# Attention and a two-layer MLP on one core: sums of x one by one, buffers of their own for the first product's sums, a stricter count of slots, twelve score groups in range two

## The chip, the cores and the metric

The kernel runs on one core of a Trainium2 chip. The metric is device time in microseconds, of the whole launch. Matmuls run on PE (TensorE), elementwise work on DVE (VectorE) and ACT (ScalarE, which also takes the exponentials and the activation), copies that change type and the loads from memory on POOL (GpSimd), stores and transposing DMAs on SP (SyncE). Each engine works through its own instructions in the order in which the program gives them; between engines semaphores hold an instruction back until what it reads is written and what it overwrites is read.

## The reference

Eight batches of attention with 12 heads, 448 positions and a head width of 64, then an MLP over the 3584 tokens, 768 wide, 2048 inside, with a leaky ReLU:

```python
scores = scale * np.matmul(q, k.transpose(0, 1, 3, 2))
attn = np.exp(scores) / (np.sum(np.exp(scores), axis=-1, keepdims=True) + 1e-09)
x = np.matmul(attn, v).transpose(0, 2, 1, 3).reshape(3584, 768)
h = x @ w_in
out = np.maximum(0.01 * h, h) @ w_out
```

(The maximum that the reference takes off the scores first is left out here.)

## The kernel before

**Attention.** Two heads make a unit; there are 48 units, six to a batch. A unit is loaded by POOL (`load_soft`, L131), cast by POOL (`cast`, L160 for q and k, L162 for v), turned on SP by a transposing DMA (`turn`, L227), and its scores come in four chunks of 112 keys. Three chunks, whatever their units, are a group: six matmuls on PE (`scores`, L261) into three score slots `sc` of PSUM, and three exponentials on ACT (`expo`, L270) into `e`. The value products of a unit are 32 matmuls (`rows`, L798, into a score slot; in the early ranges `pv`, L280, into the banks `g`). DVE divides them by the sum of the exponentials (L804 and L805, or L287 and L288) and so reads the slot out, and SP turns the result into `xT`, whose columns are tokens.

**The MLP.** The tokens are cut into eight ranges of 384 and 512 in turn. From the third on, `hidden` makes the first product and `block_pair` the second. Both replace a product of two by two blocks by seven products of blocks instead of eight, in a scheme of sums: sums of blocks of x (`mix_x`, L381 to L384, on DVE, into `x_mix` and in place into `xT`), of h (`mix_h`, L408 and L409, and L520 and L524), and of the weights, made once. In `hidden` the seven products (L436, six matmuls for each of two columns' halves) run in two chains, one in the banks `g` and one in the score slots; ACT copies a partial sum out of PSUM into a tile (L448, L456, L460), DVE adds to it (L451, L463, L466), and ACT applies the ReLU (L425, the call in `act`). In `block_pair` each of the seven products has eight matmuls of 384 columns (L508), with a place to break off after four; a step is four matmuls. DVE copies or adds the bank into an output tile (`keep` L513, `join` L516, L547), and `store` (L314) sends it out by SP, at the very end by ACT's queue too. The partial sums and the output tiles come from one pool of five buffers, `o_pool`.

**What sets the order.** The first two ranges are `mlp(0)` and `mlp(1)`, and between their steps `cluster` puts one score group each, with the value products, casts, loads and turns that go with it; `begin` says how many: clusters 9 to 18 in range one, 19 to 27 in range two. `due` holds value products that are put off. From the third range on a small planner, `events(i)`, is asked at every step of `block_pair`. It keeps a clock (`now`, 0.65 a step), a time from which each slot is free and a time from which each unit is ready, and then puts a score group (`burst`) or a unit's value products (`rows`) or nothing; `plan` says how many groups each range gets. Between the steps of `hidden` only rows are put. `advance` hands SP and POOL one turn, cast or load at a time, with its counts in `to`. The sums of x for the next range are put as one block of eight on DVE, six steps after the last rows that they need; for the third range they stand ahead of `hidden(2)`. The program's order is kept on each engine.

## Time and profile before

| | us |
|---|---|
| median of 3 runs | 403.18 (402.88 to 403.83) |
| the profiled execution, its own time | 402.84 |
| span of that execution in the trace | 400.9 |
| DVE: sums of x, normalising, copies and adds: busy | 228.9 |
| ACT busy | 261.2 |

A row of a timeline gives the start in microseconds, the duration of a run of like instructions, the engine, the line of the program, the operation, the tile written and the tiles read, the shape and the count; behind it in brackets stands how long the engine was idle before, and the instruction that released it. Names are those of the program: `g` a bank, `sc` a score slot, `h` the hidden layer, `o` an output tile. The costliest groups of the page, as busy time, mean ns of one, and idle time before it with its releaser:

```profile
L270 ACT ACTIVATE e<-sc 112x896 bf16<-112x896 f32 x192 | 163.0, 918 | 51.4 <-PE sc L261 51.0
L508 PE MATMUL g<-w_out_sb,h 128*128 128x384 bf16 x416 | 77.6, 326 | 2.4 <-DVE o L513 2.4
L261 PE MATMUL sc<-qkT 64*128 64x448 bf16 x384 | 52.3, 353 | 3.4 <-DVE x L805 2.8
```

### The profile page before, as it was taken

What the parts mean: (1) busy time and instruction counts of PE and PEld (TensorE: products, weight loads), DVE (VectorE), ACT (ScalarE), POOL (GpSimd) and SP (SyncE); (2) the same over time, 40 slices, a digit from 0 to 9 for tenths busy, and PEclk for the clock granted to TensorE, in tenths of its full rate; (3) what the DMA queues carried; (4) which work ended last, traced back from release to release, by engine and by line L of the source; (5) the groups of instructions that cost most, each with busy time, mean ns of one, the idle gap of its engine ahead of it and who ended that gap; (6) DMA issues with size and microseconds to landing.
All of it is one profiled execution on the core that took longest, in us unless ns stands there. A gap on an engine that the chain in (4) does not pass through costs nothing.

```text
span 400.9 us, 10048 instructions
## 1 busy us (share of the span) xinstructions
PE 383.9 (96%) x4088; PEld 259.0 (65%) x4088; DVE 228.9 (57%) x513; ACT 261.2 (65%) x396; POOL 142.3 (36%) x222
## 2 busy tenths in 40 slices
PE   7999999999999999988999899999999899989995
PEld 3666665545556875567855598578655795658753
DVE  3662663566666683644754646475735665473853
ACT  5998885577445678755878658758787287608600
POOL 8786763657632462543025325352022000000000
PEclk9999999999999999999999999999999999999999
DMA  9999999999994986989058897769128400411022
GB/s 132 195 201 204 203 201 127 144 171 116 130 181 113 123 107 121 150 133 198 2 76 130 159 177 94 102 154 101 25 58 161 116 11 4 113 37 55 2 78 82
DMA packets 96031, 46.98 MB, mean 117 GB/s; under 512 B 52592, under 2 KB 92656, under 8 KB 95984
## 3 DMA queue, kind: packets, MB, share of 16 engines
q0 software_dynamic: 40272, 22.58, 44.2%
q1 hardware_dynamic: 55408, 23.50, 30.4%
q8 instruction: 32, 0.52, 0.6%
q10 hardware_dynamic: 304, 0.25, 0.2%
q14 instruction: 15, 0.12, 0.1%
HBM read 45.61 MB, written 11.01 MB: 141 GB/s over the span
## 4 chain that ended last, share of the span: by engine, by line
PE 53%; DVE 6%; DMA 4%; issue 1%; ACT 1%; SPq 0%; DVEq 0%; ACTq 0%
PE g L508 22%; PE sc L436 10%; PE g L436 10%; PE sc L261 6%; PE sc L798 6%; DMA xT<-x 2%; DMA out_dram<-o 2%; DVE o L513 1%; DVE xT L382 1%; DVE x_mix L383 1%; ACT h L425 1%; DVE x_mix L381 1%; DVE x_mix L384 1%; DVE x L805 1%; DVE h L520 0%
## 5 line engine op out<-in xcount | busy, mean ns | idle before, releaser
L270 ACT ACTIVATE e<-sc 112x896 bf16<-112x896 f32 x192 | 163.0, 918 | 51.4 <-PE sc L261 51.0
L508 PEld LDWEIGHTS <-h 128*128 128x128 bf16 x632 | 57.6, 98 | 45.8 <-issue 13.1
L508 PE MATMUL g<-w_out_sb,h 128*128 128x384 bf16 x416 | 77.6, 326 | 2.4 <-DVE o L513 2.4
L425 ACT ACTIVATE h<-o 128x384 bf16<-128x384 f32 (+1 forms) x72 | 40.6, 576 | 23.5 <-DVE o L451 17.4
L261 PE MATMUL sc<-qkT 64*128 64x448 bf16 x384 | 52.3, 353 | 3.4 <-DVE x L805 2.8
L436 PEld LDWEIGHTS <-w_in_sb 128*128 128x128 bf16 x576 | 52.0, 98 | 5.4 <-issue 1.6
L160 POOL COPY qkb<-fq 112x512 bf16<-112x512 bf16 x38 | 26.3, 692 | 77.8 <-DMA qkT<-qkb 55.6
L162 POOL COPY v<-fv 112x512 bf16<-112x512 bf16 x38 | 24.8, 654 | 64.5 <-PE sc L798 32.3
L436 PEld LDWEIGHTS <-w_in_mix 128*128 128x128 bf16 x432 | 39.1, 98 | 4.6 <-issue 2.2
L508 PE MATMUL g<-w_mix,h 128*128 128x384 bf16 (+1 forms) x216 | 39.8, 320 | 1.0 <-DVE o L513 0.5
L335 PE MATMUL g<-xT,w_in_sb 128*128 128x512 bf16 (+1 forms) x180 | 36.5, 354 | 0.1
L261 PEld LDWEIGHTS <-qkT 64*128 64x128 bf16 x384 | 15.8, 94 | 30.6 <-issue 22.5
L798 PEld LDWEIGHTS <-e 112*128 112x128 bf16 x896 | 31.1, 98 | 5.3 <-ACT e L270 4.2
L798 PE MATMUL sc<-v,e 112*128 112x65 bf16 x896 | 33.4, 194 | 0.1
L516 DVE TENSOR_TENSOR o<-o,g 128x384 f32<-128x384 f32 x39 | 21.5, 551 | 20.4 <-PE g L508 20.2
L160 POOL COPY qkb<-fk 112x512 bf16<-112x512 bf16 x38 | 25.5, 670 | 13.2 <-DMA fk<-in_k_dram 13.0
L280 PEld LDWEIGHTS <-e 112*128 112x128 bf16 x640 | 23.4, 98 | 9.1 <-issue 7.2
L513 DVE COPY o<-g 128x384 f32<-128x384 f32 x39 | 21.6, 553 | 12.2 <-PE g L508 11.8
L335 PEld LDWEIGHTS <-w_in_sb 128*128 128x128 bf16 x192 | 17.9, 97 | 15.8 <-issue 0.4
L436 PE MATMUL g<-xT,w_in_sb 128*128 128x192 bf16 (+1 forms) x216 | 26.6, 259 | 1.3 <-DVE o L451 1.3
L280 PE MATMUL g<-v,e 112*128 112x65 bf16 x640 | 26.9, 194 | 0.5 <-ACT e L270 0.2
L436 PE MATMUL sc<-xT,w_in_sb 128*128 128x192 bf16 (+1 forms) x216 | 26.6, 259 | 0.0
(90 smaller groups left out, 489.9 us busy)
## 6 DMA issues: line engine op xcount, KB each, us to landing
fq<-in_q_dram POOLq DMA_DIRECT2D x19, 224.0 KB, 5.1
fk<-in_k_dram POOLq DMA_DIRECT2D x19, 224.0 KB, 6.5
fv<-in_v_dram POOLq DMA_DIRECT2D x19, 224.0 KB, 6.5
w_in_sb<-in_moe_w_in_dram POOLq DMA_DIRECT2D x4, 768.0 KB, 10.9
w_out_sb<-in_moe_w_out_dram POOLq DMA_DIRECT2D x4, 768.0 KB, 13.4
out_dram<-o SPq DMA_DIRECT2D x7, 336.0 KB, 3.6
out_dram<-o SPq DMA_DIRECT2D x8, 288.0 KB, 3.1
out_dram<-o SPq DMA_DIRECT2D x7, 240.0 KB, 3.1
```

What stands on the lines that cost most here:

```text
L160: by(qk_sb[u][:, x].rearrange("p so h d -> p h so d"), f)
L162: by(v_sb[u % NV][:, :, :, :D], f)
L261: nc.tensor.matmul(ps[:, j, :S], t[j * D:(j + 1) * D, S + c * SC:S + c * SC + P], t[j * D:(j + 1) * D, :S], start=True, stop=True,)
L270: nc.scalar.activation(e[:, :, c, :], sc_t.pop((u, c))[:SC, :, :S], AX.Exp, scale=scale)
L280: nc.tensor.matmul(ps[:, qc, :], e[:, at:at + P], vt[:, j, c, :], start=(c == 0), stop=(c == NSC - 1),)
L335: nc.tensor.matmul(open_t[m][:, :n], w_in_sb[:, kk, ts(m, P)], xT[:, kk, at:at + n], start=(fresh and kk == kks[0]), stop=(kk == KD - 1),)
L425: nc.scalar.activation(hs[:, m:m + 2, cols], x.rearrange("p (m t) -> p m t", m=2), AX.Prelu, alpha=0.01)
L436: nc.tensor.matmul(ps[:, j * nh:(j + 1) * nh], w[:, kk, ts(j, P)], x[:, kk], start=(first and j == 0 and kk == 0), stop=(kk == KH - 1), sk ...
L508: nc.tensor.matmul(ps[:, cols], x[:, m], w[:, m], start=(first and m == 0), stop=(m == MH - 1), skip_group_check=True,)
L513: nc.vector.tensor_copy(o[:, at], ps[:, :NW])
L516: nc.vector.tensor_add(o[:, at], o[:, at], ps[:, :NW])
L798: nc.tensor.matmul(ps[:, j, qc, :], e[:, at:at + P], vt[:, j, c, :], start=(c == 0), stop=(c == NSC - 1),)
```

## The change

It has five parts.

1. `mix_x` becomes a generator, `mix_x_part`, that gives one subtraction at a time. From the third range on one of them is put at a step of `block_pair`, beginning five steps after the rows that its part needs; in range two they stand in the second block pair, and the block ahead of `hidden(2)` is gone.
2. The first product's partial sums have a pool of their own, `c_pool`, with five buffers; `o_pool` has three instead of five and holds output tiles only.
3. The planner counts more strictly: a group of scores is put when its slots are free by 0.05 instead of 0.15, rows hold their slot for 1.25 instead of 1.1, and rows are put only when the next group or the next range needs them. `plan` changes to fit.
4. Range two has twelve score groups instead of nine (`begin`), and the counts that the supply begins with change with it; the cast pool has three buffers instead of four and there are five value buffers instead of six, with v casts held back in `due_v` until no value products are due.
5. The tile that warms PE up lies in `x_mix`. The last product's second half goes to a score slot, and what its bank already holds is copied out ahead and added behind.

```diff
-    cast_pool = ctx.enter_context(tc.tile_pool(name="cast", bufs=4))
+    cast_pool = ctx.enter_context(tc.tile_pool(name="cast", bufs=3))
...
-    o_pool = ctx.enter_context(tc.tile_pool(name="o", bufs=5))
+    o_pool = ctx.enter_context(tc.tile_pool(name="o", bufs=3))
+    c_pool = ctx.enter_context(tc.tile_pool(name="c", bufs=5))
...
-    NV = 6
+    NV = 5
...
-    warm = const_pool.tile([P, 512], BF16)
+    warm = x_mix.rearrange("p x k n -> p (x k n)")[:, :512]
...
+    def mix_x_part(i, ks):
...
-        nc.vector.tensor_sub(t3, xT[:, far, two], xT[:, near, two])
-        nc.vector.tensor_sub(xT[:, near, two], xT[:, near, two], xT[:, near, one])
-        nc.vector.tensor_sub(t2, xT[:, far, two], xT[:, near, two])
-        nc.vector.tensor_sub(t4, xT[:, far, one], t2)
+        for o, x, y in (
+            (t3, xT[:, far, two], xT[:, near, two]),
+            (xT[:, near, two], xT[:, near, two], xT[:, near, one]),
+            (t2, xT[:, far, two], xT[:, near, two]),
+            (t4, xT[:, far, one], t2),
+        ):
+            nc.vector.tensor_sub(o, x, y)
+            yield
...
-                return o_pool.tile([P, DM], F32, name="o")[:, :2 * nh]
+                return c_pool.tile([P, 4 * P], F32, name="c")[:, :2 * nh]
...
         if last:
+            nc.vector.tensor_copy(o2[:, NW // 2:NW], b[:, NW // 2:NW])
             store(o1, token(i, x1), left)
             store(o2, t0, right)
...
+            end = slots[0][:, 0]
+            yield from product(end, h[:, hi, two], t4[:, :, w2], first=True, cols=w2)
+            nc.vector.tensor_add(o2[:, w2], o2[:, w2], end[:, w2])
+            store(o2, t0, w2, (nc.scalar, nc.sync))
...
         mix_h(i, ready.pop())
+        x_sums = mix_x(i + 1)
...
+                if c and x > 2:
+                    next(x_sums, None)
...
-            cast(u + 3 + r)
+            cast(u + 3 + r, (0, 1))
+            due_v.append(u + 3 + r)
+        while due_v and not due:
+            cast(due_v.pop(0), (2,))
...
-    begin = [9, 8 * 2 + 3, 8 * 3 + 4]
+    begin = [9, 8 * 2 + 3, 8 * 3 + 7]
...
-    to = {"turn": 24, "cast": 24, "v": 24, "load": [26, 26, 26]}
+    to = {"turn": 26, "cast": 27, "v": 27, "load": [30, 30, 30]}
...
-        if u < min(NU, to["turn"] + 3, to["load"][0], to["load"][1]):
+        if u < min(NU, to["turn"] + 2, to["load"][0], to["load"][1]):
...
-    plan = [0, 0, 9, 9, 5, 8, 5, 0]
+    plan = [0, 0, 8, 8, 4, 8, 5, 0]
...
-                if want and not blocked and all(t <= now + 0.15 + 0.2 * x for x, t in enumerate(at)):
+                if want and not blocked and all(t <= now + 0.05 + 0.2 * x for x, t in enumerate(at)):
...
-                if whole and at[0] <= now + 0.05 and ready.get(u, 0) <= now + 0.05 and (want or u < HP * (i + 2)):
+                if whole and at[0] <= now + 0.05 and ready.get(u, 0) <= now + 0.05 and (
+                    u <= (chunk + 5) // NSC - NE or u < HP * (i + 2)
+                ):
...
-                    free[id(t)] = now + 1.1
+                    free[id(t)] = now + 1.25
...
-                if not mixed:
-                    fresh = fresh + 1 if rows_done >= HP * (i + 2) else 0
-                    if fresh > 5:
-                        mix_x(i + 1, slice(0, 2))
-                        mix_x(i + 1, slice(2, 3))
-                        mixed = True
+                for y in range(2):
+                    fresh[y] += rows_done >= HP * (i + 2) - 1 + y and 14 * c + x > 4
+                for y, sums in enumerate(x_sums):
+                    if fresh[y] > 4 and next(sums, 0) is None:
+                        break
```

On DVE, in the second product of the seventh range, the sums of x for the last range stood as one block between two copies out of the banks (`L513`, `g_99` and `g_100` are the two banks, `L381` to `L384` the sums):

```order
L516 TENSOR_TENSOR o<-o,g_100 128x384
L513 COPY o<-g_99 128x384
L381 TENSOR_TENSOR x_mix<-xT 128x512
L382 TENSOR_TENSOR xT<-xT 128x2x256
L383 TENSOR_TENSOR x_mix<-xT 128x512
L384 TENSOR_TENSOR x_mix<-xT,x_mix 128x512
L381 TENSOR_TENSOR x_mix<-xT 128x256
L382 TENSOR_TENSOR xT<-xT 128x256
L383 TENSOR_TENSOR x_mix<-xT 128x256
L384 TENSOR_TENSOR x_mix<-xT,x_mix 128x256
L513 COPY o<-g_100 128x384
```

After the change the same place reads (the sums are now L393, the copies L523, the adds L526; `g_102` and `g_103` are the banks):

```order
L523 COPY o<-g_102 128x384
L393 TENSOR_TENSOR x_mix<-xT 128x512
L393 TENSOR_TENSOR xT<-xT 128x2x256
L523 COPY o<-g_103 128x384
L393 TENSOR_TENSOR x_mix<-xT 128x512
L393 TENSOR_TENSOR x_mix<-xT,x_mix 128x512
L526 TENSOR_TENSOR o<-o,g_102 128x384
L393 TENSOR_TENSOR x_mix<-xT 128x256
L393 TENSOR_TENSOR xT<-xT 128x256
L526 TENSOR_TENSOR o<-o,g_103 128x384
```

Two sums stand between any two copies or adds where eight stood at one place.

On PE, at one place of a second product, the last value products of a unit (`L798`, or L827 after) were followed by four matmuls of the second product and then by the scores of the next group (`L261`); before:

```order
L798 MATMUL sc_102<-v_108,e_111 128x65
L508 LDWEIGHTS h
L508 MATMUL g_99<-w_mix,h 128x384
L508 LDWEIGHTS h
L508 MATMUL g_99<-w_mix,h 128x384
L508 LDWEIGHTS h
L508 MATMUL g_99<-w_mix,h 128x384
L508 LDWEIGHTS h
L508 MATMUL g_99<-w_mix,h 128x384
L261 LDWEIGHTS qkT_113
L261 MATMUL sc_101<-qkT_113 128x448
```

After, the end of the stretch between rows and scores (the second product is L518, the scores L262):

```order
L518 LDWEIGHTS h
L518 MATMUL g_103<-w_out_sb,h 128x384
L518 LDWEIGHTS hmix
L518 MATMUL g_102<-w_mix,hmix 128x384
L518 LDWEIGHTS hmix
L518 MATMUL g_102<-w_mix,hmix 128x384
L518 LDWEIGHTS hmix
L518 MATMUL g_102<-w_mix,hmix 128x384
L518 LDWEIGHTS hmix
L518 MATMUL g_102<-w_mix,hmix 128x384
L262 LDWEIGHTS qkT_115
L262 MATMUL sc_105<-qkT_115 128x448
```

Between rows and the next scores there are now at least two steps of four matmuls, and what stands there belongs to two products.

On ACT, at the end of range two, where the copies of the third range's first product begin (`L448`), one group's three exponentials (`L270`) stood there last, with value products and MLP work of PE ahead of them:

```order
L270 ACTIVATE e_112<-sc_103 112x2x448
L270 ACTIVATE e_112<-sc_102 112x2x448
L270 ACTIVATE e_112<-sc_101 112x2x448
L270 ACTIVATE e_112<-sc_103 112x2x448
L448 COPY o<-g_99 128x384
L448 COPY o<-sc_102 128x384
```

After (the exponentials are L271, the copy L458, and it writes a tile `c`):

```order
L271 ACTIVATE e_112<-sc_106 112x2x448
L271 ACTIVATE e_112<-sc_105 112x2x448
L271 ACTIVATE e_113<-sc_104 112x2x448
L271 ACTIVATE e_113<-sc_106 112x2x448
L271 ACTIVATE e_113<-sc_105 112x2x448
L271 ACTIVATE e_113<-sc_104 112x2x448
L271 ACTIVATE e_114<-sc_106 112x2x448
L458 COPY c<-g_102 128x384
```

The last two groups of range two are the last six of these exponentials, and the two groups' scores on PE have 32 value products between them.

More of the change, by code (lines that the diff above doesn't have):

```diff
@@ L372, in mix_w_in, with mix_x @@
             yield
-    def mix_x(i, ks):
+    def mix_x(i):
+        yield from mix_x_part(i, slice(0, 2))
+        yield from mix_x_part(i, slice(2, 3))
+    def mix_x_part(i, ks):
         at = cuts[i] % NX
@@ L544, in block_pair @@
         yield
-        for w in (slice(0, NW // 2), slice(NW // 2, NW)) if last else (left,):
-            yield from product(b, h[:, hi, two], t4[:, :, w], cols=w)
-            nc.vector.tensor_copy(o2[:, w], b[:, w])
-            if last:
-                store(o2, t0, w, (nc.scalar, nc.sync))
-        if not last:
-            store(o2, t0)
+        if last:
+            w1, w2 = slice(0, NW // 2), slice(NW // 2, NW)
+            yield from product(b, h[:, hi, two], t4[:, :, w1], cols=w1)
+            nc.vector.tensor_copy(o2[:, w1], b[:, w1])
+            store(o2, t0, w1, (nc.scalar, nc.sync))
+            end = slots[0][:, 0]
+            yield from product(end, h[:, hi, two], t4[:, :, w2], first=True, cols=w2)
+            nc.vector.tensor_add(o2[:, w2], o2[:, w2], end[:, w2])
+            store(o2, t0, w2, (nc.scalar, nc.sync))
+            return
+        yield from product(b, h[:, hi, two], t4)
+        keep(o2, left, b)
+        store(o2, t0)
         banks.reverse()
@@ L616, in mlp @@
                     next(sums, None)
+                if c and x > 2:
+                    next(x_sums, None)
             yield MH * NW, True
+        for _ in x_sums:
+            pass
     def supply(u):
@@ L663 @@
     due = []
+    due_v = []
     def finish(a, j):
@@ L695, in cluster @@
         if r < 3:
-            cast(u + 3 + r)
+            cast(u + 3 + r, (0, 1))
+            due_v.append(u + 3 + r)
+        while due_v and not due:
+            cast(due_v.pop(0), (2,))
+        if r < 3:
             load(u + 5 + r)
@@ L758 @@
         finish(*due.pop(0))
+    while due_v:
+        cast(due_v.pop(0), (2,))
     for _ in sums:
@@ L855, in events @@
                     now += 1.08
-                    free[id(t)] = now + 1.1
-                    if not want:
-                        break
-                    break
+                    free[id(t)] = now + 1.25
                 break
     for i in range(2, B):
-        if i == 2:
-            mix_x(i, slice(0, 2))
-            mix_x(i, slice(2, 3))
         for step, _ in enumerate(hidden(i)):
@@ L869 @@
                 rows()
-        mixed = i + 1 == B
-        fresh = 0
+        x_sums = [mix_x_part(i + 1, slice(0, 2)), mix_x_part(i + 1, slice(2, 3))] if i + 1 < B else []
+        fresh = [0, 0]
         plans = events(i)
@@ L880 @@
                 used = 0.65
-                if not mixed:
-                    fresh = fresh + 1 if rows_done >= HP * (i + 2) else 0
-                    if fresh > 5:
-                        mix_x(i + 1, slice(0, 2))
-                        mix_x(i + 1, slice(2, 3))
-                        mixed = True
+                for y in range(2):
[3 more added lines that the diff above has]
+                        break
         assert chunk >= min(3 * (START + sum(plan[:i + 1])), NU * NSC), (i, chunk)
-        if not mixed:
-            assert rows_done >= HP * (i + 2), (i, rows_done)
-            mix_x(i + 1, slice(0, 2))
-            mix_x(i + 1, slice(2, 3))
+        assert i + 1 == B or rows_done >= HP * (i + 2), (i, rows_done)
+        for sums in x_sums:
+            for _ in sums:
+                pass
 _INS = ['q', 'k', 'v', 'moe_w_in', 'moe_w_out']
```

## The prediction

> **What bounds the kernel now.** I read the shares of the engines on the page first, then PE's own timeline for its holes, and for each hole the row that ends it: the timelines of DVE, ACT and POOL, the waits and the chain that ended last.
>
> ```profile
> PE 383.9 (96%) x4088; PEld 259.0 (65%) x4088; DVE 228.9 (57%) x513; ACT 261.2 (65%) x396; POOL 142.3 (36%) x222
> ```
>
> PE (the matrix engine) is busy for 96% of the span, and no other engine for more than 65%. So only two things can shorten the kernel: less PE work, or fewer holes in PE's row. The change leaves the PE work as it is (the same 64 groups of scores, the same products), so all that it can win are holes. They are counted from the start of one group to the start of the next, less what the group takes undisturbed; the bracket alone is too small, since the pipe's end is modelled.
>
> **What the change removes.** The profiled execution took 402.84 us; the sum is made against that. The median of the runs is 403.18, 0.34 above it.
>
> *First term: the eight sums of x in one block on DVE.* At each of six places PE waits for a copy or a normalisation that stands behind the block.
>
> ```profile
> 126.37 0.74 PE L261 MATMUL sc<-qkT 64*128 64x448 bf16 x6
> 127.04 1.19 PE L280 MATMUL g<-v,e 112*128 112x65 bf16 x32
> 151.34 1.07 PE sc L798 x32
> 152.42 0.65 PE g L508 x4
> 165.51 0.55 PE L261 MATMUL sc<-qkT 64*128 64x448 bf16 x4
> 166.41 0.37 PE L261 MATMUL sc<-qkT 64*128 64x448 bf16 x2 [0.35 <-DVE x L805]
> 166.71 0.82 PE L508 MATMUL g<-w_out_sb,h 128*128 128x384 bf16 x4
> 310.49 0.35 DVE L381 TENSOR_TENSOR x_mix<-xT 128x384 bf16<-128x384 bf16 x1
> ...
> 312.98 0.55 DVE L513 COPY o<-g 128x384 f32<-128x384 f32 x1
> 311.12 1.46 PE L508 MATMUL g<-w_mix,hmix 128*128 128x384 bf16 x8
> 313.58 1.46 PE L508 MATMUL g<-w_out_sb,h 128*128 128x384 bf16 x8 [1.00 <-DVE o L513]
> 354.17 1.46 PE L508 MATMUL g<-w_mix,hmix 128*128 128x384 bf16 x8
> 357.03 1.46 PE L508 MATMUL g<-w_out_sb,h 128*128 128x384 bf16 x8 [1.40 <-DVE o L513]
> 132.68 0.66 PE L436 MATMUL sc<-x_mix,w_in_mix 128*128 128x192 bf16 x6
> 133.95 0.66 PE L436 MATMUL g<-xT,w_in_sb 128*128 128x192 bf16 x6 [0.61 <-DVE o L451]
> 268.51 0.82 PE L436 MATMUL sc<-x_mix,w_in_mix 128*128 128x256 bf16 x6
> 270.03 0.81 PE L436 MATMUL g<-xT,w_in_sb 128*128 128x256 bf16 x6 [0.71 <-DVE o L451]
> 171.98 0.55 PE L261 MATMUL sc<-qkT 64*128 64x448 bf16 x4
> 173.66 0.36 PE L261 MATMUL sc<-qkT 64*128 64x448 bf16 x2 [1.13 <-DVE x L805]
> 222.55 0.55 PE L261 MATMUL sc<-qkT 64*128 64x448 bf16 x4
> 224.40 0.37 PE L261 MATMUL sc<-qkT 64*128 64x448 bf16 x2 [1.30 <-DVE x L805]
> ```
>
> The undisturbed sizes first: a group of scores takes 0.67 (126.37 to 127.04), the two last matmuls of one that waited 0.30 (166.41 to 166.71), a product of eight 1.30 (four take 0.65 in the chain's row at 152.42); by the column that is 0.65 for six matmuls of 256 columns and 0.49 for six of 192. The block at 310.49 reads best: eight subtractions, the next copy out of a bank only at 312.98, and PE's group at 313.58 has waited for it. The holes in time's order: from 132.68, 1.27 - 0.49 = 0.78; from 171.98, 1.68 + 0.30 - 0.67 = 1.31; from 222.55, 1.85 + 0.30 - 0.67 = 1.48; from 268.51, 1.52 - 0.65 = 0.87; from 311.12, 2.46 - 1.30 = 1.16; from 354.17, 2.86 - 1.30 = 1.56. Together **7.2**. After the change one sum (0.35 by the row at 310.49) stands at a step of four matmuls, so two at a product of 1.30, with 0.55 for its copy or join: 1.25 of 1.30, and the bank is due only one product later. So I let these holes go whole; what is late next is DVE itself where a normalisation comes on top, priced below.
>
> *Second term: scores that come too soon behind rows.* "Rows" are the 32 value products, a group of scores has six matmuls and needs three score slots.
>
> ```profile
> 153.00 0.88 PE L261 MATMUL sc<-qkT 64*128 64x448 bf16 x6
> ...
> 342.24 0.88 PE L261 MATMUL sc<-qkT 64*128 64x448 bf16 x6
> ```
>
> Between ranges two and seven 18 of the 36 groups take 0.14 more (0.88 against 0.74 at 126.37; 153.00 is the first, 342.24 the last): their third slot still holds the rows, which DVE reads out. The order before puts one step (0.65, at 152.42) between rows and scores there, the order after always two or more, so the third slot is wanted 0.65 later, against 0.14 missing. That is 18 x 0.14 = 2.5, and the group at 165.51, 1.20 - 0.67 = 0.53: **3.0**. Where DVE has two sums more between, it reads the rows out some 0.7 later, and this gain is half lost; that is in the small waits below.
>
> *Third term: the output's buffers.* Twice the first product's copy on ACT needs a buffer whose store is still out.
>
> ```profile
> 184.14 0.82 PE L436 MATMUL g<-x_mix,w_in_mix 128*128 128x256 bf16 x6
> 185.79 0.82 PE L436 MATMUL sc<-x_mix,w_in_mix 128*128 128x256 bf16 x6 [0.83 <-ACT o L456]
> 187.66 0.81 PE L436 MATMUL sc<-xT,w_in_mix 128*128 128x256 bf16 x6 [0.40 <-ACT o L460]
> ACT o L456 <- DMA out_dram<-o: 1.5, 1, 1.5
> 179.73 7.19 DMA out_dram<-o
> ```
>
> 185.79 - 184.14 - 0.65 = 1.0; the group at 187.66 is the second after 185.79 and would stand at 185.79 + 2 x 0.65 = 187.09: 0.57. Together **1.6**. With buffers of their own the copies wait for DVE and ACT alone. The price would be in the outputs, which keep three buffers of five: the second pair's second tile needs the buffer of the first pair's first tile at its fourth product, so five products after the store's issue at least, 6.5 us, and this store, the one that held the chain, took 7.19. I take nothing, and as an upper bound one store late by 0.7.
>
> *Fourth term: the end.*
>
> ```profile
> 395.28 0.82 PE L508 MATMUL g<-w_mix,h 128*128 128x192 bf16 x8
> 396.55 0.82 PE L508 MATMUL g<-w_mix,h 128*128 128x192 bf16 x8 [0.45 <-DVE o L547]
> 396.53 1.64 ACTq L314 DMA_DIRECT2D out_dram<-o  x2
> ```
>
> 1.27 - 0.65 = 0.6 of hole goes (eight matmuls of 192 columns, half of a product); but the first half's stores issue until 396.53 + 1.64, and the last issue may then wait for its queue. I take **0.45**, between 0.3 and 0.6. The added copy of a partial sum (192 columns, half of the 0.55 at 312.98, some 0.3) lies beside the product before.
>
> The four terms make 7.2 + 3.0 + 1.6 + 0.45 = **12.2**.
>
> **What the change adds.** *Three more score groups in range two*, of which two pairs follow each other with few value products between, at the ends of range two's two block pairs (about 110 to 133 us).
>
> ```profile
> 126.83 2.53 ACT L270 ACTIVATE e<-sc 112x896 bf16<-112x896 f32 x3 [2.66 <-PE sc L261]
> 128.46 0.67 PE L280 MATMUL g<-v,e 112*128 112x65 bf16 x16 [0.23 <-DVE x L288]
> ```
>
> The exponentials of the group at 126.37 end 0.46 + 2.53 = 2.99 after its scores begin, and a following group uses the third slot 0.45 after its own begin (two thirds of 0.67); so two groups must lie 2.54 apart. In the first pair 48 value products lie between (0.67 + 1.5 x 1.19 = 2.45, short by 0.1; a value product also waits for DVE as at 128.46, 0.23): 0.4 with both and some more for the late exponential. In the second pair there are 32: 0.67 + 1.19 = 1.86, short by 0.7, and the 0.23 again: 0.9. Behind it the first product of the next range starts with ACT's copies queued behind the six exponentials: 0.5 to 0.9, I take 0.7. Sum **+2.0**; nothing at all if the exponentials are early, and 3 if each comes whole. The 2.5 us of exponentials themselves are no gain elsewhere, for ACT has room.
>
> *Small waits of the new order.*
>
> ```profile
> L805 DVE TENSOR_TENSOR x<-sc,rec 112x512 bf16<-112x512 f32 x28 | 19.4, 692 | 1.0
> ```
>
> A normalisation (0.69) beside two sums and a copy makes 1.94 of DVE in a product that rows stretch to 1.30 + 1.07 = 2.37; without that stretch it is 0.64 over. I take **+0.8**, one such place, between 0 and 3 (five of them).
>
> Other edits are put at nothing: POOL's and SP's supply (cast buffers three for four, value buffers five for six) has room by its rows below; the warm tile only changes its address.
>
> So 402.84 - 12.2 + 2.0 + 0.8 = 393.4, and with part of the median's 0.34 **393.6**.
>
> One row speaks for a further cost of spreading the sums.
>
> ```profile
> 129.46 1.09 POOL L162 COPY v<-fv 112x512 bf16<-112x512 bf16 x1
> 130.11 0.65 DVE L382 TENSOR_TENSOR xT<-xT 128x384 bf16<-128x384 bf16 x1
> ```
>
> One sum took 0.65 where the row at 310.49, of the same shape, has 0.35, beside a copy on POOL. Forty-eight sums lie in the six ranges; if one in eight is stretched by 0.30, that is 1.8 us of DVE, and a third of it on PE is inside the 0.8. If POOL holds one in two, it is 7.2 us, and half of it on PE would be 3.6 us, so 397. By the Trainium skill ("SBUF — State Buffer", section "SBUF: two separate sides") a DVE operation with two SBUF inputs and a GpSimd operation that reads SBUF exclude each other for the whole instruction. By that rule spread sums, which meet more copies than a block does, would come to the second of the two figures, 397; the trace shows the stretch in these rows, 0.30, and not how often it would come.
>
> **The rivals.** *Costs stay at nothing* (0.08): 402.84 - 12.2 = 390.6.
>
> *Spread sums still hold PE* (0.15). DVE works in order, and a sum that needs a transposed tile holds every copy behind it. For it: a transpose in flight has held the chain for 7.5 us.
>
> ```profile
> 163.51 7.50 DMA xT<-x
> ```
>
> Against it: that row is the longest of the chain, and the first sums begin five steps behind the rows that they need, 3.25 us and whatever rows (1.07) or scores (0.67) lie between, some 5 us, and the copy behind has a product's room, 1.30. So a landing like that one costs 7.5 - 5 - 1.3 = 1.2, a shorter one nothing. If 0.6 to 0.8 reach PE in each of five ranges, the time is about 397; with the stretch by POOL (3.6) it is the same, and both have this chance together.
>
> *Supply in range two comes late* (0.12).
>
> ```profile
> L131 POOL DMA_DIRECT2D fq<-in_q_dram x5: 701/701/703, 68.1 to 108.4; - x5
> 74.96 1.24 PE L335 MATMUL g<-xT,w_in_sb 128*128 128x512 bf16 x5
> ```
>
> Loads of a pair of units went out every (108.4 - 68.1) / 4 = 10.1 us. Range two lasts from 74.96 to its last value products at 128.46, 54 us, for nine groups or 6.75 units (four thirds of a group are a unit). Twelve groups are nine units; three groups and 2.25 units of value products more (3 x 0.67 + 2.25 x 1.19) make it 58.7 us, 6.5 per unit, while the loads come at 5.0 per unit. That is room, but the buffers are fewer and a late unit stops PE outright. Two to five us late: 396 to 398.
>
> *Slower* (0.04): the same supply as the bound. If the three cast buffers and the deferred value casts hold the loads to over 15.2 us a pair (7.6 per unit), range two grows by 9 x (7.6 - 6.5) = 9.9 and eats the gain; at 16 us a pair it is 9 x 1.5 = 13.5, and the time is about 407. From 10.1 that is far. *The order is not what the planner thinks* (0.04): slots come free elsewhere and the second term turns into waits as large, with all else as forecast: 393.6 + 3.0 + 3.0 = 399.6.
>
> **How the numbers follow.** The forecast has 0.57, with a range of its own of 391.5 to 395.5; costs at nothing 0.08, the rivals at 396 to 398 0.27, 399.6 and slower 0.04 each. The range that leaves two in ten out runs from 390.6 to 398.0. A measurement of this kernel tells about 0.2% (0.8 us) from no change: faster by more 0.92, within 0.03, slower by more 0.05.
>
> **What would show it.** Right: no sum of x behind which PE waits at the six places; all 36 score groups behind ranges two to seven at 0.67; ACT's copies without a wait for the output; the two halves of the last product 0.65 from start to start; new holes at the score groups and first products between 110 and 133 us, some 2 us in all. Wrong: holes before score groups of range two that a transpose or a cast ends (supply); sums that wait for the transposes of x, with PE behind them; holes at the stores' buffers in the second products.

## The result and the profile after

The changed kernel takes 393.52 us (median of 4 runs, 392.70 to 394.67) against 403.21 for the kernel before: the ratio is 0.976, with a 95% interval of 0.9733 to 0.9787. Run again beside later experiments it had 0.9773 (0.9743 to 0.9803). The ratios are taken over the runs within 1.5% of a kernel's fastest, which leaves out two of the twelve of one kernel below (ten groups). The profiled execution took 393.48, 9.36 less than the one before; the forecast for it was 393.4.

The page of the changed kernel, shares of the engines first, then, from its waits (us in total, times, longest), PE's for the exponentials ahead of rows:

```profile
PE 381.0 (97%) x4088; PEld 257.4 (66%) x4088; DVE 230.5 (59%) x517; ACT 260.6 (67%) x396; POOL 144.6 (37%) x222
PEld L827 <- ACT e L271: 6.2, 20, 0.7
```

No wait of ACT for a store is left among its waits. The first thing to look for in PE's timeline is the last place of the block of sums, where the kernel before had its hole of 1.56. The start of one product to the start of the next is 1.30 again, and only a small hole stands one product earlier:

```profile
343.85 1.46 PE L518 MATMUL g<-w_mix,h 128*128 128x384 bf16 x8
345.51 1.46 PE L518 MATMUL g<-w_out_sb,h 128*128 128x384 bf16 x8 [0.20 <-DVE o L526]
346.81 1.46 PE L518 MATMUL g<-w_mix,hmix 128*128 128x384 bf16 x8
```

345.51 - 343.85 - 1.30 = 0.36 comes from an add that stands on DVE behind a normalisation and a sum of h. Such a hole is not new: the kernel before had one of 0.37 two products ahead of the 1.56 (the twelve matmuls ahead of it begin at 349.25 and take 1.95, and the next begins at 351.57, released by a copy of DVE).

The end of the kernel, on PE, after the change:

```profile
386.35 0.82 PE L518 MATMUL g<-w_mix,h 128*128 128x192 bf16 x8
387.01 0.82 PE L518 MATMUL sc<-w_mix,h 128*128 128x192 bf16 x8
```

The two halves follow each other in 0.66, not 1.27. But from the last group's start to the end of the span it is 391.7 - 387.01 = 4.69, where it was 400.9 - 396.55 = 4.35 before: 0.34 of the 0.61 is given back behind PE.

The new holes are where the added groups stand, in range two: at the end of its first block pair and at its very end (PE, then ACT):

```profile
116.86 1.20 PE L281 MATMUL g<-v,e 112*128 112x65 bf16 x32
118.28 0.74 PE L281 MATMUL g<-v,e 112*128 112x65 bf16 x16 [0.22 <-DVE x L289]
...
131.05 0.74 PE L262 MATMUL sc<-qkT 64*128 64x448 bf16 x6
131.72 1.35 PE L281 MATMUL g<-v,e 112*128 112x65 bf16 x32
133.00 0.65 PE L262 MATMUL sc<-qkT 64*128 64x448 bf16 x4
134.09 0.36 PE L262 MATMUL sc<-qkT 64*128 64x448 bf16 x2 [0.44 <-ACT e L271]
135.41 0.66 PE L446 MATMUL sc<-xT,w_in_sb 128*128 128x192 bf16 x6
136.52 1.20 PE L827 MATMUL sc<-v,e 112*128 112x65 bf16 x32 [0.45 <-ACT e L271]
...
131.51 4.95 ACT L271 ACTIVATE e<-sc 112x896 bf16<-112x896 f32 x6 [2.96 <-PE sc L262]
```

At the first place the value products wait for DVE, 118.28 - 116.86 - 1.07 = 0.35 (1.07 is what 32 value products took in the chain before). At the second, six exponentials run without a pause from 131.51, and PE waits for them twice: the last two matmuls of the second group begin at 134.09, 1.09 after 133.00, where 0.45 would do; and the rows at 136.52 come 1.11 after 135.41 instead of 0.49.

One hole was in no expectation, at the beginning of the third range's second product:

```profile
152.49 1.47 PE L518 MATMUL g<-w_out_sb,h 128*128 128x384 bf16 x8
154.50 0.81 PE L518 MATMUL g<-w_mix,h 128*128 128x384 bf16 x4 [0.54 <-DVE o L523]
```

154.50 - 152.49 - 1.30 = 0.71. The last experiment is about it.

### The profile page after: what moved, and what is told of

It reads as the page before. It is cut to its first block, busy times and chain, and to the rows that moved or that the text cites. A ratio compares the mean times of both kernels' runs of the same rounds, so it can differ in the third digit from the quotient of the medians.

```text
span 391.7 us, 10029 instructions
## 1 busy us (share of the span) xinstructions
PE 381.0 (97%) x4088; PEld 257.4 (66%) x4088; DVE 230.5 (59%) x517; ACT 260.6 (67%) x396; POOL 144.6 (37%) x222
## 4 chain that ended last, share of the span: by engine, by line
PE 78%; DMA 7%; POOL 5%; issue 4%; DVE 3%; ACT 2%; DVEq 0%; POOLq 0%; ACTq 0%
PE g L518 27%; PE g L446 12%; PE sc L446 11%; PE sc L262 8%; PE sc L827 7%; PE g L336 6%; PE g L281 3%; PE g L581 3%; DMA w_mix<-in_v_dram 3%; DMA fv<-in_v_dram 2%; DMA w_in_mix<-in_k_dram 2%; POOL qkb L161 1%; POOL v L163 1%; ACT h L435 1%; ACT e L271 1%
## 5 line engine op out<-in xcount | busy, mean ns | idle before, releaser
L271 ACT ACTIVATE e<-sc 112x896 bf16<-112x896 f32 x192 | 162.7, 917 | 56.2 <-PE sc L262 56.0
L518 PEld LDWEIGHTS <-h 128*128 128x128 bf16 x632 | 57.8, 98 | 44.6 <-issue 11.5
L518 PE MATMUL g<-w_out_sb,h 128*128 128x384 bf16 x416 | 78.3, 326 | 0.3 <-DVE o L526 0.2
L435 ACT ACTIVATE h<-c 128x384 bf16<-128x384 f32 (+1 forms) x72 | 40.6, 576 | 22.5 <-DVE c L461 14.8
L161 POOL COPY qkb<-fq 112x512 bf16<-112x512 bf16 x38 | 28.2, 743 | 72.2 <-DMA qkT<-qkb 56.5
L262 PE MATMUL sc<-qkT 64*128 64x448 bf16 x384 | 49.5, 353 | 1.1 <-DVE qkT L251 0.6
L518 PE MATMUL g<-w_mix,h 128*128 128x384 bf16 (+1 forms) x208 | 38.5, 323 | 0.7 <-DVE o L523 0.5
L523 DVE COPY o<-g 128x384 f32<-128x384 f32 x51 | 28.2, 553 | 13.0 <-PE g L518 12.6
L827 PEld LDWEIGHTS <-e 112*128 112x128 bf16 x832 | 28.4, 98 | 6.5 <-ACT e L271 6.2
L827 PE MATMUL sc<-v,e 112*128 112x65 bf16 x832 | 31.1, 194 | 0.5 <-ACT e L271 0.5
L526 DVE TENSOR_TENSOR o<-o,g 128x384 f32<-128x384 f32 x39 | 21.5, 551 | 14.6 <-PE g L518 14.5
L262 PEld LDWEIGHTS <-qkT 64*128 64x128 bf16 x384 | 14.7, 94 | 23.3 <-issue 14.8
L281 PE MATMUL g<-v,e 112*128 112x65 bf16 x704 | 29.6, 194 | 0.4 <-DVE x L289 0.2
```

The costliest lines, as they stand in the source:

```text
L161: by(qk_sb[u][:, x].rearrange("p so h d -> p h so d"), f)
L262: nc.tensor.matmul(ps[:, j, :S], t[j * D:(j + 1) * D, S + c * SC:S + c * SC + P], t[j * D:(j + 1) * D, :S], start=True, stop=True,)
L271: nc.scalar.activation(e[:, :, c, :], sc_t.pop((u, c))[:SC, :, :S], AX.Exp, scale=scale)
L281: nc.tensor.matmul(ps[:, qc, :], e[:, at:at + P], vt[:, j, c, :], start=(c == 0), stop=(c == NSC - 1),)
L435: nc.scalar.activation(hs[:, m:m + 2, cols], x.rearrange("p (m t) -> p m t", m=2), AX.Prelu, alpha=0.01)
L518: nc.tensor.matmul(ps[:, cols], x[:, m], w[:, m], start=(first and m == 0), stop=(m == MH - 1), skip_group_check=True,)
```

## The experiments

Each kernel is told by its ratio to the kernel before, since the runs of that one went from 402.45 to 403.83 (medians) between the chips. Spans are those of one profiled execution each; the changed kernel had 391.7 and, when run again, 391.5. The intervals reach 0.7 to 2.1 us to each side, so a difference of under 1 us between two ratios can't be told from none without the traces.

| kernel | ratio (95%) | span, us |
|---|---|---|
| the change | 0.9760 (0.9733 to 0.9787) | 391.7 |
| the change, again | 0.9773 (0.9743 to 0.9803) | 391.5 |
| the change, sums in a block | 0.9810 (0.9787 to 0.9833) | 394.4 |
| the change, one pool of five buffers | 0.9784 (0.9764 to 0.9803) | 392.8 |
| the change, old planner | 0.9777 (0.9757 to 0.9796) | 392.9 |
| the change, old end | 0.9753 (0.9737 to 0.9770) | 392.3 |
| before, sums one at a time | 0.9836 (0.9784 to 0.9888) | 392.1 |
| the change, block and old planner | 0.9959 (0.9931 to 0.9986) | 398.3 |
| the change, nine groups and old planner | 0.9824 (0.9782 to 0.9865) | 395.6 |
| the change, twelve groups placed earlier | 0.9746 (0.9715 to 0.9777) | 389.7 |
| the change, ten groups | 0.9962 (0.9929 to 0.9995) | 405.4 |
| the change, eleven groups | 0.9811 (0.9779 to 0.9844) | 392.0 |
| earlier groups, copies by DMA | 0.9735 (0.9706 to 0.9765) | 390.1 |

### One part put back at a time

The sums in one block:

```diff
-                for y, sums in enumerate(x_sums):
-                    if fresh[y] > 4 and next(sums, 0) is None:
-                        break
+                if fresh[1] > 5:
+                    for sums in x_sums:
+                        for _ in sums:
+                            pass
```

(and in range two the two lines that put single sums are taken out)

> The changed kernel with the eight sums of x of a range in one block again, six steps after the last rows that they need, and for the third range behind range two's second block pair; all else as changed. Theory (the block on DVE holds PE, 7.2 us at six places): 393.5 + 7.2 = 400.7, from 399 to 402, with a hole of 0.8 to 1.6 us at each of the six places, ended by DVE. Rival (the gain is in the other edits, and with them DVE has room enough for a block): under 395.5.

Measured: 396.15 us, 1.5 to 2.0 over the changed kernel by the ratios (0.9810 less 0.9773 and 0.9760) and 2.7 to 2.9 by the spans. Neither end: the block costs something, but not 7.2. The timelines say why. This is the last place (PE), as bad as it was:

```profile
349.25 1.46 PE L518 MATMUL g<-w_out_sb,h 128*128 128x384 bf16 x8
352.12 1.46 PE L518 MATMUL g<-w_mix,h 128*128 128x384 bf16 x8 [1.40 <-DVE o L526]
```

And this is the fourth range, where the kernel before lost 1.48 at 222.55 (DVE, then PE):

```profile
213.07 0.35 DVE L393 TENSOR_TENSOR x_mix<-xT 128x384 bf16<-128x384 bf16 x1
...
215.81 0.69 DVE L832 TENSOR_TENSOR x<-sc,rec 112x512 bf16<-112x512 f32 x1
...
213.87 1.20 PE L825 MATMUL sc<-v,e 112*128 112x65 bf16 x32
214.91 0.81 PE L518 MATMUL g<-w_mix,h 128*128 128x384 bf16 x4
215.56 0.81 PE L518 MATMUL g<-w_out_sb,h 128*128 128x384 bf16 x4
216.30 0.74 PE L262 MATMUL sc<-qkT 64*128 64x448 bf16 x6
```

The eight sums are there from 213.07 on, and the normalisation of the rows stands behind them and ends at 216.50. But with the strict planner two steps lie between the rows and the next scores, and the third slot is wanted only at 216.30 + 0.45 = 216.75. The block is hidden. At one step it would have been wanted 0.65 earlier. The other places lie between: 0.49 and 0.78 are lost at the beginning of the third range's first product (137.84 to 140.09), 0.61 in its second (at 167.42), 0.45 at the beginning of the sixth range's first product (at 262.22), and nothing at the place of the old 313.58. On the other side, the changed kernel's 0.71 at 154.50 isn't there.

The partial sums and the outputs in one pool again:

```diff
-    o_pool = ctx.enter_context(tc.tile_pool(name="o", bufs=3))
-    c_pool = ctx.enter_context(tc.tile_pool(name="c", bufs=5))
+    o_pool = ctx.enter_context(tc.tile_pool(name="o", bufs=5))
...
-                return c_pool.tile([P, 4 * P], F32, name="c")[:, :2 * nh]
+                return o_pool.tile([P, DM], F32, name="o")[:, :2 * nh]
```

> The changed kernel with the first product's partial sums and the outputs in one pool of five buffers again. Theory (two waits of ACT's copies for a store, 1.0 and 0.57): 393.5 + 1.6 = 395.1, from 394.3 to 396, with PE waiting for ACT's copies at the beginning of a first product, and those for a store. Rival (these two waits were accidents of one execution's transfers, or the other edits already moved the stores): within 0.5 of 393.5.

Measured: 394.95 us, 0.4 to 1.0 over the changed kernel by the ratios (0.9784 less 0.9773 and 0.9760), 1.1 to 1.3 by the spans. One wait for a store that holds PE is back, in another range than before (the waits, then PE):

```profile
ACT o L457 <- DMA out_dram<-o: 1.6, 1, 1.6
239.82 0.66 PE L445 MATMUL sc<-xT,w_in_sb 128*128 128x192 bf16 x6
241.60 0.66 PE L445 MATMUL g<-x_mix,w_in_mix 128*128 128x192 bf16 x6 [1.12 <-ACT o L457]
```

241.60 - 239.82 - 0.49 = 1.29. A shared pool makes such a wait possible, not sure: the kernel below with the split alone shares it too, and its waits name no store.

The planner's old numbers:

```diff
-                if want and not blocked and all(t <= now + 0.05 + 0.2 * x for x, t in enumerate(at)):
+                if want and not blocked and all(t <= now + 0.15 + 0.2 * x for x, t in enumerate(at)):
...
-                    u <= (chunk + 5) // NSC - NE or u < HP * (i + 2)
+                    want or u < HP * (i + 2)
...
-                    free[id(t)] = now + 1.25
+                    free[id(t)] = now + 1.1
```

> The changed kernel with the planner's old numbers (0.15, 1.1, rows also when groups are still wanted), but the new numbers of groups for each range. 19 score groups then stand one step behind rows instead of none. Theory (third slot late by 0.14): 19 x 0.14 = 2.7, so 396.2, from 395.5 to 397.5, and the groups take 0.80 to 0.84 again. Rival (it is the smaller number of groups in the later ranges that brought the gain): under 394.5, the groups at 0.67.

Measured: 394.78 us, between the theory and the rival: 0.2 to 0.7 over by the ratios, 1.2 to 1.4 by the spans. The mechanism is as expected: 19 of the groups of scores take 0.87 or 0.88 in PE's timeline from 150 us on and 14 take 0.74, while in the changed kernel all 33 take 0.74. 19 x 0.14 = 2.7 should be lost, and only half of it or less is. Some of it is a trade. With two steps ahead of the scores, the rows stand close behind them, and PE waits for their exponentials (the waits of this kernel, to hold against the 6.2 and 20 above):

```profile
PEld L827 <- ACT e L271: 4.4, 16, 0.7
```

That is four waits and 1.8 of weight loads' idle time, part of it beside matmuls. In PE's own timeline, summed from start to start from the third range's second product on, 2.5 more is lost behind the 33 groups of scores (2.64 for 0.11) and 0.75 less ahead of the 21 rows that stand behind the second product (0.82 for 1.57). So the trade leaves 1.8 by the trace, of which the spans show 1.2 to 1.4; the rest isn't settled.

The old end (the last product's second half in the first's bank):

```diff
-            end = slots[0][:, 0]
-            yield from product(end, h[:, hi, two], t4[:, :, w2], first=True, cols=w2)
-            nc.vector.tensor_add(o2[:, w2], o2[:, w2], end[:, w2])
...
+        for w in (slice(0, NW // 2), slice(NW // 2, NW)) if last else (left,):
+            yield from product(b, h[:, hi, two], t4[:, :, w], cols=w)
+            nc.vector.tensor_copy(o2[:, w], b[:, w])
```

(and the copy ahead is taken out)

> The changed kernel with the last product's second half in the bank of the first again. Theory: the hole of 0.6 on PE is back, and the last store lands 0.3 to 0.6 later: 393.8 to 394.1. Rival (the issue of the first half's stores sets the end in both): no difference, the hole is back but the span from PE's last matmul to the end is shorter by as much.

Measured: 393.86 us, ratio 0.9753 beside 0.9760 and 0.9773: no difference that can be told. The spans differ by 0.6 to 0.8, but the runs don't show it. In its trace the hole is back (386.68 to 387.95, 1.27 for 0.66), and from the last group's start to the end it is 392.3 - 387.95 = 4.35 again. So the trace has the theory's hole and a part of what the rival names, a shorter way to the end: the change of the end is worth 0.61 - 0.34 = 0.27 there; whether it is worth anything in the time stays open.

The four parts put back alone cost 1.5 to 2.0, 0.4 to 1.0, 0.2 to 0.7 and nothing by the ratios: less than half of the 9.7. So the parts don't add up, and the next three kernels ask how.

### How the parts work together

The first part alone, in the kernel before (the changed kernel's generator and its places for the sums; nothing else):

> The kernel before with the first part of the change alone: the sums of x one at a time, as the changed kernel places them. With the block put back, the changed kernel lost 2.0 us, not 7.2. Theory A (two of the six holes are removed by the split and by other parts alike, so that each alone is enough): here all six holes go, ratio to before 0.982 to 0.986 (5.6 to 7.2 us faster), with no hole of over 0.5 behind a sum of x. Theory B (the sums held PE for 2 us only, and the rest came by other parts): ratio 0.994 to 0.996.

Measured: ratio 0.9836 (0.9784 to 0.9888), 6.6 us faster, with runs from 393.86 to 397.86 (the profiled execution was the fastest of the four, by 2.0, so the span in the table flatters this kernel). That is theory A: the split alone removes the six holes. But for the old end's 0.61, the longest that PE has left from the third range on is 0.41, at a group behind rows (171.22).

The block and the planner's old numbers, both put back:

> The changed kernel with the block of sums and the planner's old numbers together. If parts add up: 2.0 + 0.7, ratio 0.983 (from 0.981 to 0.985). If the planner's stricter count is what removed the holes that the block made at 222.55 (1.48) and 313.58 (1.16) and half of the one at 173.66: these are back, ratio 0.988 to 0.993.

Measured: 401.22 us, ratio 0.9959 (0.9931 to 0.9986), 7.5 to 8.0 us over the changed kernel, where the two alone cost 1.5 to 2.0 and 0.2 to 0.7. That is more than either expected range allows. Of the holes that were expected the one at the place of the old 313.58 is back:

```profile
308.82 1.46 PE L518 MATMUL g<-w_mix,hmix 128*128 128x384 bf16 x8
311.30 1.46 PE L518 MATMUL g<-w_out_sb,h 128*128 128x384 bf16 x8 [1.01 <-DVE o L523]
```

311.30 - 308.82 - 1.30 = 1.18. Behind rows PE waits for a copy at 265.30 too (0.49), and the third range has 0.60 and 0.31; but in place of the old 1.48 in the fourth there is only 0.27. So a block on DVE costs PE when something stands close behind it, and the strict planner removes much of what stands close: the spread of the sums removes the holes whole, the strict count more than half of them, and put back one by one the two look small. The spans say the same with less: 394.4 and 392.9 alone, 398.3 together, where the two alone would add up to 395.7. How much of the larger figure of the ratios is more than the spread of the runs (400.09 to 402.56, the fastest of them profiled) isn't settled.

Nine groups in range two with the planner's old numbers:

```diff
-    begin = [9, 8 * 2 + 3, 8 * 3 + 7]
+    begin = [9, 8 * 2 + 3, 8 * 3 + 4]
...
-    plan = [0, 0, 8, 8, 4, 8, 5, 0]
+    plan = [0, 0, 9, 9, 5, 8, 5, 0]
```

(with the counts `to` of the kernel before, and the planner's numbers as two kernels above)

> The changed kernel with nine score groups in range two and the planner's old numbers, nine, nine, five, eight and five groups in the ranges after (the strict count finds no room for so many). Theory (twelve groups cost 1.3 us at range two's end and gain only what the planner's count needs): the two places at range two's end are gone (1.3 to 1.7 faster), the late third slots are back (1.0 slower, as the old numbers alone showed): ratio 0.974 to 0.977. Rival (twelve groups in range two carry most of the gain that the other parts put back one by one don't explain, some 6 us): ratio 0.985 or more.

Measured: 395.67 us, ratio 0.9824 (0.9782 to 0.9865): neither, 2.1 to 2.6 us slower than the changed kernel. (Its profiled execution was the slowest of the four, by 1.5.) The price is in DVE, and then on PE, at the fifth range:

```profile
256.63 0.42 DVE L393 TENSOR_TENSOR x_mix<-xT 128x512 bf16<-128x512 bf16 x1 [2.89 <-DMA xT<-x]
...
256.89 0.55 PE L262 MATMUL sc<-qkT 64*128 64x448 bf16 x4
258.42 0.36 PE L262 MATMUL sc<-qkT 64*128 64x448 bf16 x2 [0.97 <-DVE x L834]
```

A sum of x waits 2.89 for a transpose, the normalisation of the rows stands behind it (at 257.68), and the scores behind that. It is the rival of the spread sums that hold PE, in another kernel than the one it was named for.

### Range two, and a version that is faster than both

The groups of range two put earlier:

```diff
-        total = MD * KD * n + 2 * 7 / 4 * MD * DM
+        total = (MD * KD * n + 2 * 7 / 4 * MD * DM) * (0.92 if i else 1)
```

> The changed kernel with range two's twelve groups put a little earlier (the total of work by which they are placed is taken 8% smaller), so that seven instead of six stand in its first product and one instead of two behind each other at its end. Theory (two groups behind each other at range two's end cost PE 0.14 + 0.18 + 0.70 + 0.61 by the changed kernel's timeline): 1.2 to 1.6 faster than the changed kernel beside it, no hole of over 0.3 between 128 and 138. Rival (the supply bounds range two: units are wanted every 5.0 us there, as fast as the loads come): no gain or a loss, with holes before scores or value products that a cast or a turn ends.

Measured beside the changed kernel on one chip: 391.93 us (391.5 to 393.08, 6 runs) against 393.21 (392.49 to 393.9, 6 runs), 1.28 faster, as the theory has it but for one clause: a hole of a little over 0.3 is left. PE at range two's end now:

```profile
131.97 1.20 PE L281 MATMUL g<-v,e 112*128 112x65 bf16 x32
133.39 0.66 PE L446 MATMUL g<-xT,w_in_sb 128*128 128x192 bf16 x6 [0.22 <-DVE x L289]
```

One group stands there (at 131.30, ahead of these value products), the hole left is 133.39 - 131.97 - 1.07 = 0.35, and the supply follows although the groups come closer. The rival falls.

The changed kernel beside it:

> The changed kernel itself once more, as the measure for the three beside it: ratio to before 0.973 to 0.979.

Measured: 0.9773, within.

Ten groups in range two (`begin` 8 * 3 + 5, `plan` 8, 8, 4, 8, 7 for ranges three to seven) and eleven (8 * 3 + 6; 8, 8, 4, 8, 6), with the counts `to` that belong to them:

> The changed kernel with ten groups in range two and seven in the seventh range instead of five. Theory (a group costs nothing in the seventh range, and the pair of groups at range two's very end is gone, while that at the end of its first pair of blocks has 32 value products between instead of 48): 0.3 to 1.3 faster than the changed kernel beside it. Rival (DVE's sums and rows in the seventh range leave no room for two more groups): slower by 0.3 or more, with holes behind 300.

> The changed kernel with eleven groups in range two and six in the seventh range. Theory: one pair at range two's first end is gone, worth 0 to 0.4, the pair at its very end stays: 0 to 0.4 faster than the changed kernel beside it. Rival as with ten groups: slower.

Measured: ten groups 401.81 us (397.73 to 407.2), ratio 0.9962; eleven 394.46 us, ratio 0.9811, 1.25 over the changed kernel beside them. Both theories fall. The rivals are right that it is slower, but not why: with eleven groups PE has no hole of over 0.2 in the seventh range. The holes are in the fourth and fifth (eleven groups; waits, DVE, then PE; the first DVE row is the changed kernel's, for comparison):

```profile
DVE x_mix L393 <- DMA xT<-x: 13.1, 6, 3.3
232.97 0.69 DVE L834 TENSOR_TENSOR x<-sc,rec 112x512 bf16<-112x512 f32 x1
...
247.89 0.69 DVE L834 TENSOR_TENSOR x<-sc,rec 112x512 bf16<-112x512 f32 x1
...
254.18 0.85 DVE L393 TENSOR_TENSOR x_mix<-xT 128x512 bf16<-128x512 bf16 x1 [3.31 <-DMA xT<-x]
...
253.91 0.81 PE L518 MATMUL g<-w_out_sb,h 128*128 128x384 bf16 x4
255.55 0.81 PE L518 MATMUL g<-w_mix,h 128*128 128x384 bf16 x4 [0.82 <-DVE o L526]
```

Six sums wait for transposes, 13.1 us in all; the changed kernel's waits have no such line. The add that releases PE at 255.55 stands on DVE behind the sum of 254.18. The reason is the lead of the scores. The first sum for the sixth range needs the rows of the 35th unit, which is whole with 140 chunks. By `begin` and `plan`, 47 groups or 141 chunks are done when the fifth range begins with twelve groups, 46 or 138 with eleven, 45 or 135 with ten. So in the changed kernel those rows are put in the fifth range's first product, and their normalisation begins at 232.97, 21 us ahead of the sum (at 254.18 too). With eleven groups they come only in the second product, at 247.89, and the sum five steps behind them waits for a transpose that is still on its way, until 254.18. The kernel with nine groups and the old numbers has 138 chunks there as well: its normalisation begins at 250.63, and the sum waits until 256.63.

The profiled execution with ten groups is the slowest of its twelve (407.2), so its sizes don't hold for the others. It fails in the same way: five of its sums wait for transposes, 11.1 in all, PE itself waits 3.73 for one, at 266.37, and there holes stand behind 300 too.

### Sums beside copies on POOL

The last kernel is the one with earlier groups, and in it the q and k copies of units 28 and 29 are made by DMAs:

```diff
-                by(qk_sb[u][:, x].rearrange("p so h d -> p h so d"), f)
+                o = qk_sb[u][:, x].rearrange("p so h d -> p h so d")
+                if u in (28, 29):
+                    for y in range(2):
+                        nc.gpsimd.dma_start(out=o[:, y], in_=f[:, y])
+                else:
+                    by(o, f)
```

> The kernel with range two's groups put earlier, with the q and k copies of units 28 and 29 made by DMAs that POOL issues instead of by POOL itself. In the kernel without this, four such copies lie between 144.7 and 150.1, beside DVE's sums of h, of which four took 0.64 to 1.24 instead of 0.42, and PE then waits 0.92 at 152.57. Theory (the copies on POOL stretch the sums, and these hold PE): sums of h between 144 and 152 back at 0.42 to 0.45 where only DMA issues lie beside them, the hole at the beginning of the third range's second product under 0.4, and 0.3 to 0.8 faster than the 391.9 of the kernel without it (ratio 0.973). Rival (the sums are slow for another reason, or the late activations on ACT set that hole): sums still over 0.6 and the hole 0.7 or more.

The same stretch without the DMAs (earlier groups; POOL, DVE, PE):

```profile
148.73 0.62 POOL L161 COPY qkb<-fq 112x512 bf16<-112x512 bf16 x1
149.28 0.83 POOL L161 COPY qkb<-fk 112x512 bf16<-112x512 bf16 x1
148.40 1.24 DVE L418 TENSOR_TENSOR hmix<-h 128x512 bf16<-128x512 bf16 x1
149.74 0.64 DVE L419 TENSOR_TENSOR h<-h 128x512 bf16<-128x512 bf16 x1
150.34 1.47 PE L518 MATMUL g<-w_out_sb,h 128*128 128x384 bf16 x8
152.57 1.46 PE L518 MATMUL g<-w_mix,h 128*128 128x384 bf16 x8 [0.76 <-DVE o L523]
```

And with them:

```profile
148.05 1.41 POOL L164 DMA_DIRECT2D qkb<-fk  x2
150.15 0.63 POOL L168 COPY v<-fv 112x512 bf16<-112x512 bf16 x1
149.34 0.43 DVE L423 TENSOR_TENSOR hmix<-h 128x512 bf16<-128x512 bf16 x1
150.21 0.86 DVE L423 TENSOR_TENSOR hmix<-h 128x512 bf16<-128x512 bf16 x1
151.51 1.47 PE L523 MATMUL g<-w_out_sb,h 128*128 128x384 bf16 x8
152.92 1.46 PE L523 MATMUL g<-w_mix,h 128*128 128x384 bf16 x8
```

Seven of the eight sums take 0.42 or 0.43; the one that meets the copy left on POOL, at 150.15, takes 0.86. The hole on PE shrinks from 152.57 - 150.34 - 1.30 = 0.93 to 0.11. The theory holds for the cause. It fails for the time: 392.11 us, ratio 0.9735 beside 0.9746, no difference that can be told. In its profile a hole of 0.67 stands in range two at 109.83 that the kernel without has not, which is about what was won; whether the DMAs cause it was not tried.

## Why the prediction was right, step by step

**The time.** 393.4 was worked out for the profiled execution, and it took 393.48. The sum is that good because it was made for all parts together, from holes that are in fact gone, and both of its halves come out in PE's timelines. Of the 12.2 that were to go, all went: the six holes (7.2), 2.7 behind the groups of scores and the 0.53 at 165.51, the two waits for a store (1.6) and 0.27 at the end make 12.3. Against the 2.8 that were to come stand 2.9: 1.5 in range two, 0.71 at 154.50 and 0.7 ahead of rows. The spans differ by 400.9 - 391.7 = 9.2. But the terms are not what each part is worth by itself.

**The block of sums, 7.2.** Right in the size and the mechanism: the six holes are gone, and the part alone in the kernel before brings 6.6 (4.5 to 8.7). What the prediction didn't see is that the second term's planner would have removed more than half of them by itself: with the strict count the block costs 1.5 to 2.9. One size in the working was small: a sum of 512 columns takes 0.42 where the working took 0.35 from one of 384, so two of them and a copy make 1.39 of a product's 1.30; PE shows no hole for it.

**Scores behind rows, 3.0.** The mechanism is right, all 33 groups are at 0.67 again (three of the 36 are now in range two). Put back alone it is worth less: the old numbers cost 0.2 to 0.7 by the ratios and 1.2 to 1.4 by the spans. The step that failed is the one that let 18 x 0.14 go without a price. What came in exchange, PE's waits for exponentials ahead of rows (0.87 in all before, 1.57 after, from the third range's second product on), was in no term.

**The output's buffers, 1.6.** Right in kind, on the high side: with one pool a wait of 1.29 is back, and the time is 0.4 to 1.0 longer; but the split alone had already moved the two waits of before away. That three output buffers cost nothing was right.

**The end, 0.45.** The hole of 0.61 is gone on PE, 0.34 of it comes back behind PE, so 0.27 by the trace and nothing measurable in the time.

**Range two's groups, +2.0.** 1.8 by the trace: 0.35 at the first pair, and 0.21 at 133.00, 0.64 at 134.09 and 0.62 at 136.52 at the second; 1.5 when the 0.35 that range two's end had before (128.46 - 127.04 - 1.07) is taken off. The kernel that takes the second pair apart is 1.28 faster. For the first pair 0.4 was set, part of it for late exponentials; there the wait for DVE is all, and behind it the exponentials are not late.

**Small waits, +0.8.** Too small, 1.4 by the trace: 0.71 at 154.50, and the 0.7 ahead of rows. The one at 154.50 has a cause that the prediction had only for sums of x: sums of h stretched by POOL's copies. Five of them take 0.64 to 0.83 there; the cause was tried in the kernel with earlier groups, not in the changed kernel itself. For the sums of x the open question is answered: nine of the 48 are stretched in the changed kernel, by 2.65 us in all, nearer to the prediction's one in eight (1.8) than to its one in two (7.2). PE shows it in one hole of over 0.2, 0.29 at 130.43, behind a sum that took 0.77 at 129.15.

By the Trainium skill ("SBUF — State Buffer", "SBUF: two separate sides") a DVE operation with two SBUF inputs and a GpSimd operation that reads SBUF exclude each other for the whole instruction. The trace agrees for nine of the eleven sums of 128x512 that have a copy beside them in the changed kernel: seven begin while a copy runs and end 0.26 to 0.29 behind its end (0.64 to 0.83 in all), and two begin ahead of their copy and take 0.42 and 0.43, while the copy takes 0.72 and 0.83 instead of 0.62. The other two (at 99.68 and 148.15) it doesn't explain. The 49 sums without a copy beside them take 0.41 to 0.43. So the stretch is there as the rule has it, but too few sums meet a copy for the 397 that the prediction drew from it.

**The rivals.** Late supply didn't come, not even with groups closer together; a sign of it is the hole of 0.71 that a value cast ends at 131.01 in the profile of the kernel with the old end. Spread sums that wait for transposes didn't come in the changed kernel, but came with nine and eleven groups, and in the one profile with ten. The prediction took the twelve groups for a cost only. What they are for, the lead that the spread sums need, was not seen. (The strict count with nine groups was not run.)

## What to carry to other kernels

Count the holes of the engine that bounds, each with the row that ends it, and sum them for the whole change; but don't read a part's worth off its term, for a block of work on one engine and a consumer placed close behind it make one hole together, and removing either can remove most of it. Before a wait is spread out over an engine that works in order, look at when its inputs land: single sums are safe only as long as the producer keeps a lead, and one group less of lead (eleven for twelve) cost 1.25 us here. And where two parts each look worth little, put both back at once before calling them useless: 1.5 to 2.0 and 0.2 to 0.7 alone made 7.5 to 8.0 together.

## What was not expected of the hardware

A sum of two SBUF tiles on DVE that begins while POOL copies ends 0.26 to 0.29 after the copy does, and its row shows the wait as part of its duration: 0.64 to 0.86 us in place of 0.42 in the rows named above. One that begins ahead of the copy keeps its 0.42, and the copy takes longer. For DMA issues by POOL it is open: in the kernel with DMAs the sums beside them stayed at 0.42 or 0.43, but the sum of 1.24 in the kernel without began 0.33 ahead of its copy, while POOL issued a load.
